# Threshold attention and an ELU feed-forward block in one kernel: two more second-FFN products split once more, ELUs of two groups held back, two quarters behind the last values, a new early order

## The chip, the cores and the metric

The kernel runs on one core of a Trainium2 chip. The metric is device time in microseconds, the median of several executions; a profiled execution beside them gives the trace. Engines are named as in the profile: PE is TensorE (matmul, and PEld its weight load), DVE is VectorE, ACT is ScalarE, POOL is GpSimd, SP is SyncE, which here only issues transfers. All arithmetic is float32.

## The reference, cut to what matters

```python
# q, k, v: (8, 8, 576, 64)
scores = q @ k^T / sqrt(64)
scores = where(scores >= max(scores) - tau, scores, -1e9)
attn = exp(scores - max(scores)); attn /= sum(attn) + 1e-9
x = (attn @ v).transpose(0, 2, 1, 3).reshape(4608, 512)
h = x @ w_in                                # 512 -> 2048
g = where(h > 0, h, exp(min(h, 0)) - 1)     # ELU
out = g @ w_out                             # 2048 -> 512
```

## The kernel before

Each of the 8 sequences has 8 heads, worked as 4 head pairs; there are 32 pairs in all. A pair's scores (L493 early, L766 later) go to PSUM, DVE takes the row maximum (L517, L773), ACT the exponential (L527, L783), DVE the mask with the row sum (L537, L787), DVE, POOL and ACT sum and normalize. The squares are transposed on DVE (L640), stored to DRAM (`there`) and fetched back in another layout (`wTa`, `wTb`, L684). The values product (L818, L826) multiplies them by v, and ACT copies it to `xt` (L432), the transposed input of the FFN.

The FFN works on groups of tokens. Both of its products are computed as seven half-size products instead of eight (a Strassen scheme), with sums of input blocks and weight blocks prepared ahead. `first_product(g, u)` (matmuls at L1444) gives one of eight pieces of h of group g; ACT copies three of the seven partial results (L1458) and two blocks of h (L1505, L1506), POOL and DVE combine, and per half c ACT takes the exponential (L1474), POOL or ACT subtracts one (L1484, L1486), and DVE finishes the ELU (L1494). `second_round(g, r)` (L1584) is the second FFN product of half the hidden columns; its left operands need sums s1 to s4 of ELU results (`sums`, L1531).

The stages in time:

- Early (0 to about 263 us): the list `EARLY` is a written-out order of steps, each with an engine or a choice of engines (`:act`, `:dve`, `:pool`), carried out by `early_tasks` and `follow`. Its names: `su` row sums, `rest` parts of the weight conversion (L280 to L321), `max`, `exp`, `mask`, `th` the softmax steps, `part`/`put` transposes by PE and their copies, `half` halves of first FFN products.
- Steady state (263 to 1036 us): for pair `pr` from `START` = 9 to 32, an agenda sorted by planned time (`at`) issues each step. `tail_step` and `wide_step` give the attention work of a pair with its planned times; between them `ffn_quarters(n)` issues n quarters of FFN work (a quarter is two matmul calls, four instructions on PE). `MOVED` shifts planned times by name ("f" or "s" for a pair with first products or second rounds beside it, then the step), `FIRST` the times of one pair, or, with the key "e:" and the number of a quarter, of the steps behind the steady state.
- The last values (about 1066 to 1071 us): the values of the last pair and their copy to `xt`, from which the last two groups, 7 and 8, start.
- The last two groups: eight first products of group 7; deep round 0; first products 0 to 3 of group 8; deep round 1; first products 4 to 7; deep rounds 2 and 3. Rounds 0 and 1 are the second FFN product of group 7 (r = 0, 1), rounds 2 and 3 of group 8.

A deep round goes through seven products m in the order `DEEP` = 0, 3, 2, 4, 1, 5, 6; with four rounds that makes 28, numbered q. Each is either plain (`plain_product`, L2020: 8 calls of 128x256 columns) or split once more by the same scheme (`deep_product`, L1958: 14 calls of 128x128). Each call is two instructions on PE in the trace. A product is plain when (r, m) is in `WHOLE`, or q is 27.

A split product needs four left sums of ELU results (`level2_sum`, L1893; s1, s2, s3, s4; s3 and for r = 0 s4 on POOL, the others on DVE, unless `ON` says otherwise) and four sums of weights (`weigh`, made ahead, kept in DRAM as `there_w` and loaded by `load_weights`, L1883). Its results leave PSUM in parts: L1970, L1977, L1980 on DVE when r = 1, partly copies on ACT when r = 0; those of a plain product by L2026 on DVE when r = 1. `between(q)` issues the sums s1 and s2 of the next product and, at some places, `later_sum` (L1876, L1878). `sums_deep` (L1864, L1866) makes sums of ELU results as soon as two ELUs are done. In both kinds of sum PE waits if they are late.

The set `patient` names first products whose ELUs are planned later than usual:

```python
patient = {(B - 1, 7), (B, 3), (B, 7)}
at(now[0] + (2.0 if c and attending[0] else 1.4) + (7.0 if deep_sums and (g, u) in patient else 0.0), lambda: elu(c), f"e{v}{c}")
```

With B = 8 these are u = 7 of group 7, which runs directly before deep round 0, u = 3 of group 8 before round 1, and u = 7 of group 8 before round 2. An ELU that has not been issued yet is also issued when its buffer is taken again by a later exponential, or when a product needs its result (`ready`).

Of the kernel before, what the change touches and what calls it, by code (L numbers as in the profile page):

```python
# [60 lines left out]
ld.tail.1.0 ld.tau.0.0:act ld.k.0.1 ld.k.0.0:act idle17@f0 ld.q.0.0 ld.k.1.0 ld.k.1.1 lw.0 lw.1 tau first.t.k.0@f0  # L61
ld.k.2.0 copy.k.0 ld.k.2.1 first.k.0.0@f2 ld.k.3.0 idle4@f0 prep.k.0.0 ld.k.3.1 first.q.0.0@f0 first.q.1.0@f2
prep.q.0.0 ld.tail.0.0 first.t.k.1@f1 sc.0 copy.k.1:dve lw.2 first.t.k.2@f0 max.0.0 copy.k.2 prep.q.1.0 first.q.2.0@f0
idle7@t max.0.1 exp.0.0 th.0.0 lw.3 first.k.1.0@f2 prep.q.2.0 th.0.1 exp.0.1 mask.0.0 rest.0:pool idle5@f0 prep.k.1.0
mask.0.1 first.t.k.3@f1 ld.vd.3.0 shift.0 sc.1 copy.k.3:dve sign.0 ld.q.1.0 shift.1 su.0 ld.q.2.0 rec.0 first.q.3.0@f0
max.1.0 norm.0.0 ld.vd.0.1 prep.q.3.0 first.k.2.0@f0 max.1.1 ld.v.1.1 exp.1.0 th.1.0 rest.1:pool ld.q.3.0
first.t.q.0@f2 exp.1.1 part.0.0@t mask.1.0 th.1.1 add.0 first.k.3.0@f1 prep.k.2.0 mask.1.1 first.t.q.1@f0 ld.v.0.0
su.1:act copy.q.0 sc.2 end.0 norm.0.1:act rec.1 shift.2 prep.k.3.0 norm.1.1 part.0.1@f2 max.2.0 sign.1 idle21@f1
rest.2:pool ld.v.0.1 max.2.1 exp.2.0 th.2.0 ld.vd.0.0 th.2.1 exp.2.1 mask.2.0 add.1 lw.4 put.0.0 mask.2.1 sign.2
norm.1.0 end.1 rest.3 sc.3 ld.v.1.0 su.2:act copy.q.1 add.2 put.0.1 lw.5 part.0.2@t turn.0 max.3.0 part.1.0@f1  # L70
ld.vd.2.1 put.0.2 landed.0 first.q.0.1@f0 max.3.1 exp.3.0 th.3.0 ld.v.3.1 first.q.1.1@f2 part.1.1@t rec.2 ld.v.2.1
th.3.1 exp.3.1 mask.3.0 norm.2.0 ld.vd.1.1 prep.q.0.1 mask.3.1 ld.vd.1.0 put.1.1 part.1.2@f0 turn.1 put.1.0 shift.3
# [12 lines left out]
exp.8.1 add.8 part.6.0@t part.7.1@f1 put.7.0 mask.8.1 part.6.1@f2 sign.7 part.7.2@f0 turn.7 su.8 put.6.0 sc.9 end.7
put.7.1 end.8 lw.11 rest.9 half.0@f1 rec.8 load.k.4 shift.9 put.6.1 max.9.0 add.9 norm.8.1:act put.7.2:dve landed.7
exp.9.0 max.9.1 part.6.2@t turn.6 th.9.0 val.3.block.1@f0 norm.8.0:act th.9.1 mask.9.0 lw.12 rest.10:pool exp.9.1
shift.10 sc.10 mask.9.1 out.3.block.1 add.10 sign.9 put.6.2:dve landed.6 sign.10 part.8.0@f0 max.10.0 su.9:act
part.8.1@t part.8.2@f2 turn.8 end.9 half.1 exp.10.0 th.10.0 rec.9 put.8.2 lw.13 put.8.1 mask.10.0 norm.9.0 put.8.0
landed.8 end.10 norm.9.1 su.10:act first.t.q.3@f2 first.t.q.2@f0 sc.11 copy.q.2 copy.q.3 shift.11 lw.14 rest.11 rec.10  # L90
norm.10.0 fexp.0.0.0 val.2.block.1@t max.11.0 max.11.1 exp.11.0 th.11.0 fmin.0.0.0 exp.11.1 out.2.block.1:dve
part.10.0@f0 th.11.1 mask.11.0 add.11 part.9.0@t put.10.0 part.9.1@f2 mask.11.1 sign.11 part.10.1@f0 turn.10 shift.12
end.11 sc.12 put.10.1 landed.10 rest.12 shift.13 lw.15 sign.12 su.11:act add.12 half.4@f0 max.12.0 put.9.0 rec.11
max.12.1 exp.12.0 th.12.0 end.12 th.12.1 rest.13 part.9.2@t turn.9 half.5 exp.12.1 mask.12.0 add.13 lw.16 put.9.2
load.q.4 put.9.1 landed.9 mask.12.1 sign.13 sc.13 elu.0.0.0 norm.11.1:act su.12 rec.12 val.0.1@t norm.12.0:act
norm.12.1 max.13.0 end.13 exp.13.0 th.13.0 fexp.0.1.0 mask.13.0 norm.11.0:act fmin.0.1.0 turn.12 su.13:act rest.14
in.0.0:pool sc.14 rest.15 in.0.1:pool rec.13 send.12 in.0.2:pool part.11.0@f1 max.14.0 half.8@f2 in.1.0:pool max.14.1
exp.14.0 th.14.0 elu.0.1.0 th.14.1 lw.17 out.0.1 put.11.0 shift.15 part.11.1@f0 shift.14 exp.14.1 part.11.2@t turn.11
half.2@f1 add.14 mask.14.0 sign.14 put.11.1 mask.14.1 landed.12 norm.13.0:act end.14 sc.15 shift.16 lw.18 put.11.2:dve
landed.11 part.13.0@f0 max.15.0 half.3 max.15.1 exp.15.0 th.15.0 add.15 su.14 sign.15 rec.14 mask.15.0 rest.16 th.15.1  # L100
part.13.1@t turn.13 end.15 exp.15.1 add.16 sc.16 put.13.0 prep.q.4 put.13.1 landed.13 half.9 sign.16 mask.15.1
load.q.5 in.1.1:pool norm.14.1:act max.16.0 in.1.2:pool su.15:act shift.17 val.1.1@t exp.16.0 th.16.0 in.2.0:pool
prep.k.4 fexp.0.0.1 insend.0 rest.18:pool norm.14.0:act mask.16.0 lw.19 rest.17 end.16 fmin.0.0.1:act add.17 su.16
rec.15 lw.20 shift.18 sc.17 out.1.1 rec.16 elu.0.0.1 norm.15.1:act norm.15.0 fexp.0.0.2 part.14.0@t max.17.1 norm.16.0
half.6@f0 put.14.0 max.17.0 in.2.1:pool fmin.0.0.2:act turn.15 exp.17.0 th.17.0 th.17.1 part.14.1@t add.18 sign.17
part.14.2@f1 turn.14 half.7 exp.17.1 send.15 mask.17.0 in.2.2:pool put.14.2 mask.17.1 elu.0.0.2 part.16.0@f1 su.17:act
sign.18 end.17 sc.18 put.16.0 rec.17 end.18 lw.21 norm.17.0:act half.10@f1 max.18.0 put.14.1 landed.14 max.18.1
landed.15 exp.18.0 th.18.0 lw.22 in.3.0 th.18.1 exp.18.1 half.11 mask.18.0 rest.19:pool in.3.1:pool mask.18.1 su.18
# [68 lines left out]
def kernel(  # L177
# [13 lines left out]
    B, H, S, D = q.shape  # L191
# [29 lines left out]
    early, late = ExitStack(), {}  # L221
# [743 lines left out]
    NP = B * NPAIR  # L965
# [414 lines left out]
    with tc.manual_schedule():  # L1380
# [42 lines left out]
        def first_product(g, u):  # L1423
            r, v = divmod(u, RU)
# [704 lines left out]
```

## Time and profile before

| | before |
|---|---|
| time, median of 3 executions (lowest to highest) | 1270.01 us (1269.47 to 1270.43) |
| profiled execution, its own time | 1268.97 us |
| span of the profile (first to last instruction) | 1266.9 us |
| busy: PE / DVE / POOL / ACT | 1249.4 / 1066.1 / 790.1 / 584.1 us |
| mean granted PE clock | 0.999 |
| PE time by line on the chain of waits | L1444 31%, L1584 23%, L766 8%, L826 8%, L1958 4%, L2020 2% |

A row of a timeline is: start, duration, engine, line, operation, tiles written <- read, shapes, count; in brackets the engine's idle time before it, and who ended it. Rows with a count above 1 join instructions that follow each other. A row by stretch gives busy time per engine within a stretch of the span. In the chain of waits each row is one link: start, length, engine, tile, line, count. Line numbers are those of the kernel before; in the kernel after they are higher by 1 (by 2 from about L1999).

### The profile page before, as it was taken

The numbers are of one execution on the slowest core, as the hardware profiler recorded it, in microseconds if no ns is written. First come the engines' busy times: TensorE is split into PE (matmuls) and PEld (weight loads), VectorE is DVE, ScalarE is ACT, GpSimd is POOL, SyncE is SP. The second block draws the span as 40 slices with busy tenths as digits, with TensorE's granted clock in tenths as the row PEclk, the third lists the DMA queues.
The fourth block names the chain that finished last, engine by engine and source line by source line (L and its number), as shares of the span: only waits on it lengthen the run. The fifth ranks groups of instructions, "written<-read, shape, count | busy, mean of one in ns | idle before, by whom it ended". The sixth has DMA issues, their size and how long they took to land.

```text
span 1266.9 us, 22594 instructions
## 1 busy us (share of the span) xinstructions
PE 1249.4 (99%) x7163; PEld 992.5 (78%) x7163; DVE 1066.1 (84%) x2330; ACT 584.1 (46%) x1271; POOL 790.1 (62%) x1144
## 2 busy tenths in 40 slices
PE   7999999999999999999999999999999999999998
PEld 6776576478788887878788878878887888888898
DVE  6998989898889979898889888988989776776776
ACT  6986755453444435352625353443535251434130
POOL 5674544586576747684767657675757474775564
PEclk9999999999999999999999999999999999999999
DMA  9568898998889887988889897988898876334433
GB/s 224 144 177 237 228 260 240 246 299 214 258 205 279 216 245 213 269 238 245 234 226 264 219 267 204 268 214 253 207 279 222 243 217 241 137 125 150 135 112 113
DMA packets 332871, 277.70 MB, mean 219 GB/s; under 512 B 201296, under 2 KB 288336, under 8 KB 332752
## 3 DMA queue, kind: packets, MB, share of 16 engines
q1 hardware_dynamic: 331760, 275.73, 77.9%
q8 instruction: 57, 0.93, 0.3%
q10 hardware_dynamic: 992, 0.53, 0.2%
q14 instruction: 62, 0.51, 0.1%
HBM read 178.85 MB, written 97.32 MB: 218 GB/s over the span
## 4 chain that ended last, share of the span: by engine, by line
PE 79%; DVE 3%; issue 0%; SPq 0%; ACT 0%; DMA 0%; POOL 0%; DVEq 0%; ACTq 0%
PE f L1444 31%; PE f L1584 23%; PE sc L766 8%; PE sc L826 8%; PE f L1958 4%; PE f L2020 2%; PE sc L818 1%; PE sc L813 1%; PE f L953 1%; DVE mx L773 0%; DVE x L640 0%; DVE w_one L787 0%; DMA there<-x 0%; DVE kT L1893 0%; DVE s L1866 0%
## 5 line engine op out<-in xcount | busy, mean ns | idle before, releaser
L773 DVE TENSOR_REDUCE mx<-sc 128x1 f32<-128x576 f32 x252 | 179.9, 750 | 35.5 <-PE sc L766 28.4
L783 ACT ACTIVATE w_one<-sc,mx 128x576 f32<-128x576 f32 x140 | 101.1, 739 | 125.6 <-DVE mx L773 104.5
L779 POOL TENSOR_SCALAR th<-mx,ntau 128x2 f32<-128x2 f32 (+1 forms) x140 | 41.7, 298 | 174.5 <-DVE mx L773 174.4
L766 PE MATMUL sc<-kT,qT 64*128 64x256 f32 (+5 forms) x896 | 126.6, 418 | 2.1 <-ACT xt L432 0.9
L766 PEld LDWEIGHTS sc<-kT,qT 64*128 64x128 f32 x896 | 99.3, 186 | 35.4 <-issue 18.9
L1444 PE MATMUL f<-xt,sw 128*128 128x256 f32 x512 | 123.8, 384 | 0.5 <-ACT xt L432 0.5
L1444 PE MATMUL f<-x,w_in_sb 128*128 128x256 f32 x512 | 122.8, 382 | 0.0
L1444 PE MATMUL f<-xt,w_in_sb 128*128 128x256 f32 x512 | 121.2, 379 | 0.5 <-DVE xt L1053 0.5
L787 DVE SCALAR_TENSOR_TENSOR w_one<-sc,th,w_one 128x576 f32<-128x576 f32 x140 | 109.7, 811 | 13.1 <-ACT w_one L783 12.9
L783 ACT ACTIVATE e<-sc,mx 128x576 f32<-128x576 f32 x112 | 82.7, 742 | 74.5 <-DVE mx L773 72.2
L640 DVE STREAM_TRANSPOSE x<-w_one 128x512 f32<-128x512 f32 (+1 forms) x140 | 100.0, 744 | 15.2 <-POOL w_one L501 10.2
L501 POOL TENSOR_SCALAR w_one<-w_one,rs 128x576 f32<-128x576 f32 x115 | 89.3, 787 | 37.3 <-DVE rs L551 37.3
L1444 PEld LDWEIGHTS f<-xt,sw 128*128 128x128 f32 x512 | 94.1, 190 | 19.5 <-issue 4.3
L1444 PEld LDWEIGHTS f<-x,w_in_sb 128*128 128x128 f32 x512 | 96.2, 190 | 16.1 <-ACT g L1505 3.6
L1444 PEld LDWEIGHTS f<-xt,w_in_sb 128*128 128x128 f32 x512 | 97.2, 190 | 14.0 <-ACT e L783 0.8
L787 DVE SCALAR_TENSOR_TENSOR e<-sc,th,e 128x576 f32<-128x576 f32 x112 | 87.8, 809 | 8.2 <-ACT e L783 7.9
L1584 PE MATMUL f<-w_out_sb,g 128*128 128x256 f32 x384 | 92.0, 382 | 0.0
L1584 PE MATMUL f<-w_out_sb,s 128*128 128x256 f32 x384 | 91.9, 382 | 0.0
L1584 PE MATMUL f<-t,s 128*128 128x256 f32 x384 | 90.7, 379 | 0.0
L501 POOL TENSOR_SCALAR e<-e,rs 128x576 f32<-128x576 f32 x92 | 67.7, 741 | 35.4 <-DVE rs L551 32.6
L1584 PEld LDWEIGHTS f<-w_out_sb,g 128*128 128x128 f32 x384 | 72.0, 190 | 12.2 <-issue 2.9
L1584 PEld LDWEIGHTS f<-w_out_sb,s 128*128 128x128 f32 x384 | 72.0, 190 | 11.8 <-issue 2.5
(344 smaller groups left out, 2902.7 us busy)
## 6 DMA issues: line engine op xcount, KB each, us to landing
there<-x SPq DMA_DIRECT2D x452, 144.0 KB, 3.9
wTb<-there SPq DMA_DIRECT2D x58, 576.0 KB, 6.2
wTa<-there SPq DMA_DIRECT2D x55, 576.0 KB, 4.8
sw<-win_sums SPq DMA_DIRECT2D x62, 384.0 KB, 4.3
t<-wout_sums SPq DMA_DIRECT2D x45, 512.0 KB, 5.2
there<-x SPq DMA_DIRECT2D x112, 80.0 KB, 1.9
wTb<-there SPq DMA_DIRECT2D x56, 160.0 KB, 3.6
wst<-in_moe_w_in_dram SPq DMA_DIRECT2D x16, 512.0 KB, 4.6
```

The source lines that it names most:

```text
L501: nc.gpsimd.tensor_scalar(wv, wv, st["rs"][:, h : h + 1], 1.0, ALU.mult, ALU.mult)
L640: nc.vector.transpose(x[:, :, c0 : c0 + nc_], src.rearrange("p (c g n) -> p g c n", c=nc_, n=T))
L766: on_banks(nc.tensor.matmul(o, qT[r, i * P : (i + 1) * P], kT[r, k0 : k0 + n], start=True, stop=True, skip_group_check=True), o)
L773: on_banks(nc.vector.tensor_reduce(st["mx"][:, h : h + 1], st["sc", h], axis=AX.XY if i == NC else AX.X, op=ALU.max, negate=True), st["sc" ...
L779: nc.gpsimd.tensor_scalar(st["th"][:, cs], st["mx"][:, cs], -1.0, ntau, ALU.mult, ALU.add)
L783: on_banks(nc.scalar.activation(st["e", h], st["sc", h], AF.Exp, bias=st["mx"][:, h : h + 1]), st["sc", h])
L787: on_banks(nc.vector.scalar_tensor_tensor(st["e", h], st["sc", h], st["th"][:, h : h + 1], st["e", h], ALU.is_ge, ALU.mult, accum_out=st[" ...
L826: on_banks(nc.tensor.matmul(o, vm[:, h, c], parts[part][:, g0:g1, h * (NC + 1) + c], start=False, stop=(c == NC - 1), skip_group_check=Tru ...
L1444: nc.tensor.matmul(loc["banks"][place], left[:, j], right[:, j], start=(begins and j == 0), stop=(j == 1), skip_group_check=True)
L1584: nc.tensor.matmul(place(m), lhs, rhs, start=(begins and v == 0), stop=(v == RU - 1), skip_group_check=True)
L1958: nc.tensor.matmul(loc["x"][place][:, :P], left[:, v], right[:, v], start=(begins and v == 0), stop=(v == 1), skip_group_check=True)
L2020: nc.tensor.matmul(loc[c][:, :HM], lefts(g, r, c, m)[:, v], rights(r, m)[:, v], start=(v == 0), stop=(v == RU - 1), skip_group_check=True)
```

## The change

1. `WHOLE` loses (1, 4): the products m = 4 of rounds 1 and 3 (q = 10 and 24) are split. Split products go from 17 to 19 of 28, plain ones from 11 to 9.
2. `patient` becomes a table: the ELUs of (7, 7) and (8, 3) are held back by 20.0 instead of 7.0, those of (8, 7) by 7.0 as before.
3. The last second round leaves two quarters (four L1584 calls, eight instructions on PE) until after the last values. As side effects two of its sums (L1531) move from POOL to DVE, and the "e:" keys of `FIRST` name other quarters than before.
4. In a split product the slots run 1, 5, 6 instead of 1, 6, 5 (5 uses s1, 6 uses s2); the load of the weight sums and `later_sum` move from slot 5 to slot 6.
5. `ON` gets nine entries that put single sums on another engine; `FIRST` gets one entry, and nine planned times in `MOVED` change.
6. `EARLY` is a new order. PE's own order in the early stage is the same; 24 steps change engine and some steps of DVE, ACT, POOL and SP change places.

In the built programs, DVE has 2044 instructions before and 2063 after, ACT 1279 and 1284, POOL 1149 in both, SP 1369 and 1374; L1958 goes from 238 to 266 calls and L2020 from 88 to 72.

```diff
 FIRST = {
-    "9:3.0": 0.61, "9:turn4": 2.44, ...
+    "9:3.0": 0.61, "9:fetch0": -3.6, "9:turn4": 2.44, ...
 ON = {
+    "L8.0.0.3": 1, "S1.3": 0, "S15.2": 0, "S16.1": 1, "S16.3": 0, "S19.3": 0, "S2.3": 0, "S5.1": 1, "S5.3": 0,
 }
-WHOLE = {(0, 0), (1, 0), (0, 4), (1, 4), (1, 5)}
+WHOLE = {(0, 0), (0, 4), (1, 0), (1, 5)}
 MOVED = {
-    ... "f20.1": 2.47, ... "f26.1": 0.42, ... "f5.1": 4.32, ... "fout1": 0.83, ... "s21.0": 0.22,
-    ... "sexp11": -0.09, ... "sfetch4": 0.31, ... "sprep1": -0.32, ... "sturn4": -1.49,
+    ... "f20.1": 3.18, ... "f26.1": -0.14, ... "f5.1": 3.93, ... "fout1": 0.47, ... "s21.0": 0.51,
+    ... "sexp11": -0.16, ... "sfetch4": -0.76, ... "sprep1": -2.36, ... "sturn4": -3.1,
 EARLY = """
-... shift.0 sc.1 copy.k.3:dve sign.0 ld.q.1.0 shift.1 su.0 ld.q.2.0 rec.0 first.q.3.0@f0 ...
+... shift.0 ld.vd.3.0 sc.1 su.0:act copy.k.3:dve sign.0 ld.q.1.0 shift.1 rec.0 rest.0 ld.q.2.0 norm.0.0 ...
...
-        patient = {(B - 1, 7), (B, 3), (B, 7)}
+        patient = {(B - 1, 7): 20.0, (B, 3): 20.0, (B, 7): 7.0}
...
-                at(now[0] + (2.0 if c and attending[0] else 1.4) + (7.0 if deep_sums and (g, u) in patient else 0.0), lambda: elu(c), f"e{v}{c}")
+                at(now[0] + (2.0 if c and attending[0] else 1.4) + (patient.get((g, u), 0.0) if deep_sums else 0.0), lambda: elu(c), f"e{v}{c}")
...
-                ffn_quarters(HALF_QUARTERS)
+                ffn_quarters(HALF_QUARTERS - (2 if pr == NP and half else 0))
...
             one = [(0.1, first), (0.15, s_(q, 2))]
-            six = [(0.1, u2), (0.15, first_too), (0.35, s_(q, 3))]
-            five = [(0.2, lambda: load_weights(q + 3, 0))] + between(q)
+            b_ = between(q)
+            five = [x for x in b_ if x[0] == 0.3]
+            six = [(0.1, u2), (0.15, first_too), (0.35, s_(q, 3)), (0.2, lambda: load_weights(q + 3, 0))] + [x for x in b_ if x[0] != 0.3]
...
-            return [slot(1, one), slot(6, six), slot(5, five)], [slot(2, [(0.1, c11)]), ...], [slot(7, seven)]
+            return [slot(1, one), slot(5, five), slot(6, six)], [slot(2, [(0.1, c11)]), ...], [slot(7, seven)]
```

More of the change, by code (lines that the diff above doesn't have):

```diff
@@ L86 @@
[L86 to L95, printed above, removed]
@@ new lines @@
+put.17.1 sign.21 part.19.1@t turn.19 in.5.0 add.22 part.17.2@f1 turn.17 half.12@f2 put.19.1 landed.19 end.21 put.17.2
+landed.17 in.5.1 in.5.2:pool val.3.1@t shift.23 insend.5 sign.23 insend.4 rest.23 lw.25 sign.22 add.23 copy.k.4:act
+end.22 prep.k.5 rest.24:pool lw.26 out.3.1 t tail.4 half.19 bmax.4.4.0 insend.2 shift.24 bexp.4.4.0 bth.4.4 add.24
+sign.24 bmask.4.4.0 idle3@f1 end.23 bsu.4.4:act wsc.4.0.0 brec.4.4 end.24 lw.27 bnorm.4.4.0:act wsc.4.0.1 insend.3
+shift.25 rest.25 lw.28 bmax.4.0.0 half.16@f1 insend.1 bmax.4.0.1 bexp.4.0.0 load.q.6 bturn.4.4 bth.4.0 sign.25
@@ L2006, in deep_product @@
             slot = lambda k, posts: (lambda: p(k), posts, SLOT)
-            return [slot(1, one), slot(6, six), slot(5, five)], [slot(2, [(0.1, c11)]), slot(4, [(0.1, c21), (0.2, lambda: load_weights(q + 3, 1))]), slot(3, three)], [slot(7, seven)]
+            return [slot(1, one), slot(5, five), slot(6, six)], [slot(2, [(0.1, c11)]), slot(4, [(0.1, c21), (0.2, lambda: load_weights(q + 3, 1))]), slot(3, three)], [slot(7, seven)]
         def plain_product(q):
```

201 lines of the change are left out of this document (103 added, 98 removed), and 18 rows, old and new, of the table MOVED.

## The prediction

> **What bounds the kernel now.** I read the page's head, then busy time by stretch, the waits of TensorE (PE), the chain of waits, and the timeline around each wait.
>
> ```profile
> span 1266.9 us, 22594 instructions
> PE 1249.4 (99%) x7163; PEld 992.5 (78%) x7163; DVE 1066.1 (84%) x2330; ACT 584.1 (46%) x1271; POOL 790.1 (62%) x1144
> ```
>
> PE is busy all but 17.5 us, so a gain can only be fewer matmul-microseconds or a PE wait that goes. Where is the idle time? The view by stretch (stretch, its length, then busy time of PE, weight load, DVE, ACT, POOL, granted clock, DMA share, GB/s):
>
> ```profile
> 0.00:27.00 27.00, 20.93 (x136) 16.01 (x136) 16.32 (x43) 17.80 (x38) 13.56 (x35) 1.00 1.01 226
> 27.00:46.00 19.00, 18.32 (x171) 13.82 (x171) 17.91 (x44) 18.39 (x37) 12.71 (x19) 1.00 0.57 167
> 46.00:115.00 69.00, 67.52 (x526) 53.45 (x522) 62.19 (x143) 60.63 (x132) 45.87 (x63) 1.00 0.68 177
> 115.00:263.00 148.00, 145.03 (x708) 88.13 (x709) 130.66 (x280) 85.20 (x164) 78.44 (x109) 1.00 0.91 246
> 263.00:1036.00 773.00, 772.98 (x4334) 622.42 (x4335) 677.43 (x1490) 342.31 (x749) 507.09 (x761) 1.00 0.87 240
> 1066.00:1072.00 6.00, 5.53 (x42) 3.11 (x42) 3.26 (x7) 1.05 (x4) 0.00 (x0) 1.00 0.78 276
> 1120.00:1143.00 23.00, 21.73 (x159) 20.20 (x158) 18.81 (x42) 5.02 (x15) 16.44 (x17) 1.00 0.34 116
> 1143.00:1167.00 24.00, 24.00 (x122) 21.34 (x121) 14.91 (x31) 10.70 (x26) 12.38 (x17) 1.00 0.48 162
> 1169.00:1192.00 23.00, 22.28 (x151) 20.50 (x150) 21.55 (x57) 1.15 (x2) 13.25 (x16) 1.00 0.29 92
> 1238.00:1258.00 20.00, 20.00 (x143) 18.94 (x143) 17.86 (x48) 0.27 (x1) 9.07 (x10) 1.00 0.36 106
> ```
>
> PE idles 6.07 + 0.68 + 1.48 + 2.97 = 11.2 us in the early stage, 0.02 in the long steady state (263 to 1036), 0.47 behind the last values, 1.27 in deep round 0 (1120 to 1143), 0.72 in round 1 (1169 to 1192) and none in round 3. So the new planned times of the steady state can gain nothing; they can only lose.
>
> **The change, part by part.**
>
> *Two more products split* (L1958 instead of L2020, m = 4 in rounds 1 and 3). Rates, from the chain of waits (start, time, engine, line, count):
>
> ```profile
> 1249.98 2.68 PE f L1958 x24
> 1252.65 1.73 PE f L2020 x8
> ```
>
> A plain product issues 8 calls, each two instructions on PE: 16 at 1.73/8 = 216 ns, 3.46 us. A split one issues 28 at 2.68/24 = 112 ns, 3.13 us. Two of them save 2 x 0.33 = 0.67 us. A rule against it stands in the Trainium skill, "TensorE: Matmul & The Clock Gate", section "Back-to-back issue gap": sustained spacing is set by weight load and matmul together, about 81 ns at 128 columns and 131 ns at 512, so halving the width does not halve the time. The trace disagrees for 256 to 128: 216 ns to 112. What it would cost is the last rival.
>
> *ELUs held back 20 instead of 7* (u = 7 of group 7, u = 3 of group 8). Round 0, DVE and PE (start, time, engine, line, operation, tiles, shapes; in brackets the idle time before it and who ended it), then round 1:
>
> ```profile
> 1128.52 1.64 DVE L1494 SCALAR_TENSOR_TENSOR wTb<-km,wTb 128x512 f32<-128x512 f32 x1
> 1130.60 0.97 DVE L1866 TENSOR_TENSOR s<-wTb 128x256 f32<-128x256 f32 x1
> 1131.49 0.41 DVE L1893 TENSOR_TENSOR kT<-g 128x256 f32<-128x256 f32 x1
> 1131.83 0.41 DVE L1864 TENSOR_TENSOR e<-s,wTb 128x256 f32<-128x256 f32 x1
> 1132.16 0.68 DVE L1494 SCALAR_TENSOR_TENSOR wTa<-ge,wTa 128x512 f32<-128x512 f32 x1
> 1132.77 0.41 DVE L1893 TENSOR_TENSOR kT<-kT,g 128x256 f32<-128x256 f32 x1
> ...
> 1131.62 0.61 PE L1958 MATMUL f<-t,g 128*128 128x128 f32 x4
> 1133.23 1.16 PE L1958 MATMUL f<-x,kT 128*128 128x128 f32 x8 [1.00 <-DVE kT L1893]
> ...
> 1180.46 0.68 DVE L1494 SCALAR_TENSOR_TENSOR g<-km,g 128x512 f32<-128x512 f32 x1
> 1181.06 0.41 DVE L1893 TENSOR_TENSOR kT<-kT,wTb 128x256 f32<-128x256 f32 x1
> 1181.53 1.16 PE L1958 MATMUL f<-x,kT 128*128 128x128 f32 x8 [0.57 <-DVE kT L1893]
> ```
>
> In both rounds the second left sum (kT, L1893), which PE waits for, comes right behind an ELU (L1494) and the sums of h that the ELU sets off (L1866, L1864). These are for the next round of the same group's columns, a first-product stage later; held 20 they land in that stage (1143 to 1167), where DVE is busy 14.91 of 24. Lateness is more than the idle shown: four matmuls from 1131.62 take 0.45, so the next was due at 1132.07 and came 1.16 late, 0.16 more than the 1.00 shown, because a stopped PE drains its last matmul before it counts as idle. PE restarts five times in the two rounds, idle 1.27 + 0.72 = 1.99, so late by 1.99 + 5 x 0.16 = 2.8. DVE work ahead of these sums falls by at least 1.64 + 0.97 + 0.41 + 0.68 = 3.7 in round 0, more than any single wait. I take **-2.8** (bounds -2.8 and 0).
>
> *New DVE work.* A split product in rounds 1 and 3 adds on DVE three left sums (L1893), one L1970, six L1980, one L1977, and drops two L2026; the fourth sum goes to POOL or DVE as ON says. Groups on DVE in round 3 (busy, mean ns, idle before):
>
> ```profile
> L1980 DVE TENSOR_TENSOR ot<-f,wTb 128x128 f32<-128x128 f32 x10 | 2.8, 286 | 0.6 <-PE f L1958 0.5
> L1893 DVE TENSOR_TENSOR kT<-kT,e 128x256 f32<-128x256 f32 x2 | 1.7, 862 | 0.1
> L2026 DVE TENSOR_TENSOR kT<-f,kT 128x256 f32<-128x256 f32 x2 | 0.8, 410 | 0.0
> ```
>
> With 0.41 for an undisturbed L1893 (1131.49), and the two forms without a row here at the price of their shape (L1970 as L1980, L1977 as L2026): 3 x 0.41 + 0.29 + 6 x 0.29 + 0.41 - 2 x 0.41 = 2.9 by durations; successive rows start 0.07 sooner than that (1131.49 to 1131.83 is 0.34), nine more instructions give 0.6 back, so 2.2 us. Round 1 loses ELU work of about that size. Round 3 doesn't: 17.86 + 2.2 = 20.1 us of DVE in the 19.67 us that PE would need. So DVE is full and at least 0.4 comes out as waits; the same L1893 at 862 ns shows that a sum can take 0.45 longer. I take **+0.8** (0.4 and one stretched sum). Bounds: 0, if the tail after the last matmul takes the excess, and 3.1, if all six new L1893 stretch by 0.45 (2.7 + 0.4). The order 1, 5, 6 in place of 1, 6, 5 gives s2 one slot of four matmuls (0.45 us) more and s1 as much less; s1 is issued first and is the earlier of the two, so I take nothing for it; if s1 were the late one, it costs up to 0.45 in a round, within these bounds.
>
> *Two quarters behind the last values.* The chain, and the switch:
>
> ```profile
> 1041.75 24.37 PE f L1584 x112
> 1067.24 4.05 PE sc L826 x32
> ...
> 1069.37 1.90 PE L826 MATMUL sc<-wTa,vm 128*64 128x256 f32 x16
> 1071.31 0.37 ACT L432 COPY xt<-sc 128x256 f32<-128x256 f32 x1 [1.03 <-PE sc L826]
> 1071.74 1.56 PE L1444 MATMUL f<-xt,sw 128*128 128x256 f32 x6 [0.47 <-ACT xt L432]
> ...
> 1055.31 0.43 SPq L684 DMA_DIRECT2D wTb<-there  x1
> ```
>
> PE ends the values, the copy to xt (0.37) follows, PE waits 0.47 and is late by 0.47 + 0.16 = **0.63**. Eight L1584 matmuls (24.37/112 x 8 = 1.74 us) now fill that gap. Their sums (L1531) go from POOL to DVE, which has 3.26 of 6 busy there: hidden, else at most the 0.63 again. The values start 1.74 earlier, at 1041.75 + 24.37 - 1.74 = 1064.4; the last fetch was issued at 1055.31. No row shows the landing of this one; PE waits for no fetch now, so it lands by 1066.1 at the latest, and the step then loses up to 1.7. I take no loss.
>
> *Early stage.* PE's order stays the same; 24 entries change engine (seven row sums leave DVE for ACT, four weight conversions go from ACT to POOL) and some are reordered. The largest wait that I can follow:
>
> ```profile
> 61.02 0.71 ACT L280 ACTIVATE wst<-wst 128x512 f32<-128x512 uint32 x1
> 62.23 1.36 ACT L527 ACTIVATE e<-sc,mx 128x576 f32<-128x576 f32 x2
> 64.18 0.41 PE L554 MATMUL f<-ident,w 128*64 128x128 f32 x2 [0.55 <-ACT wTb L432]
> ```
>
> L280 there goes to POOL, so ACT reaches the exponentials up to 0.71 sooner and the 0.55 can go. Elsewhere ACT gets work in front of its exponentials. Much of the 11.2 us is start-up that no order removes. I take **-0.7**, one such wait with its 0.16; bounds -2.0 (three such) and +1.0 (ACT late once before two of PE's restarts).
>
> *Steady state, ON, SP.* 0: PE never waits there, and each moved step has other work of PE in front. SP gets one more store and four more half loads, three products ahead of their use. No row prices them; the step that waits would be one L1958 start, 0 to 0.45.
>
> Sum: -0.67 - 2.8 + 0.8 - 0.63 - 0.7 = -4.0. The profiled execution took 1268.97 (span 1266.9 and 2.07 around it), 1.04 below the median of 1270.01. So 1268.97 - 4.0 = 1264.97 as profiled, **1266.0** as a median.
>
> **Rivals.**
> (a) DVE becomes the bound of rounds 1 and 3: the new sums cost 3.1, not 0.8, so 1268.3. For it: 17.86 of 20 busy, and L1893 at 862 ns; against it: PE had no wait at all in round 3.
> (b) The held ELUs do not clear the rounds (they are also forced when their buffer is taken again), or other DVE work takes their place ahead of kT: the 2.8 stays, 1268.8. Against: the first-product stage that takes the buffer begins after the round.
> (c) Slower: a wait that repeats in the steady state. In one stage ACT has this order now:
>
> ```profile
> 474.70 0.37 ACT L1506 COPY g<-f 128x256 f32<-128x256 f32 x1 [0.49 <-PE f L1444]
> 474.97 0.63 ACT L1474 ACTIVATE ge<-g 128x512 f32<-128x512 f32 x1
> 475.63 0.63 ACT L1486 ACTIVATE ge<-ge 128x512 f32<-128x512 f32 x1
> ```
>
> The change puts L1474 and L1486 ahead of the L1506 copy, which frees a PSUM bank. The copy comes up to 1.26 - 0.49 = 0.77 later. It decides if PE needs that bank within 0.77 of now; fully so, 12 such stages cost 12 x 0.55 = 6.6: 1272.6. Against it: three banks rotate, and PE shows 0.02 idle in 773 us.
> (d) The 128-wide matmuls of the new products stay at 216 ns (weight load busy 18.94 of 20): 28 x 0.216 - 3.46 = 2.6 each, 5.2 in place of -0.67: 1271.9. By the skill's 81 to 131 ns, an estimate of some 180 ns, it would be 1269.8. Against it: 24 in 2.68.
>
> **How the numbers follow.** Forecast 0.60; (a) 0.16, (b) 0.12, (c) 0.10, (d) 0.02. The likeliest one's own range is 1264.2 to 1267.6 (early stage -2.0 to +0.5, DVE 0 to 1.6). To leave out no more than 0.2 it reaches over (a) and (b): 1264.0 to 1269.5. A measurement of this kernel tells 0.2% (2.5 us) from no change: faster is below 1267.5, slower above 1272.5. Faster: 0.57 of the forecast's, 0.09 of (a) and (b) where they come halfway: 0.66. Slower: (c) fully and a little of (d): 0.08. Same: 0.26.
>
> **What would show it.** Right: L1584 x8 between the last values and L1444 with no idle; L1494 absent from rounds 0 and 1, and kT's sum no longer ending PE's waits; 28 L1958 per new product in 3.13; PE idle in round 3 below 1. Wrong: PE idle above 0.1 between 263 and 1036; L1893 as the releaser in round 3 for over 1.5 us; early stage idle above 12; a fetch as releaser of the last values.

## The result, and the profile after

| | before | after |
|---|---|---|
| median (lowest to highest, 9 executions each) | 1269.47 us (1268.44 to 1270.43) | 1266.24 us (1265.8 to 1266.88) |
| ratio, with its 95% interval | | 0.9976 [0.9965, 0.9986] |
| span of the profile | 1266.9 us | 1264.1 us |

The change makes the kernel 3.2 us faster; the forecast was 1266.0. The page of the kernel after, its head:

```profile
span 1264.1 us, 22671 instructions
PE 1248.2 (99%) x7187; PEld 993.1 (79%) x7187; DVE 1075.3 (85%) x2349; ACT 583.7 (46%) x1276; POOL 787.1 (62%) x1144
```

PE has 24 more instructions and 1.2 us less to do; its idle time went from 17.5 to 15.9 us, DVE gained 9 us. The view by stretch (columns as in the prediction; stage boundaries have moved, so the late stretches lie 2 to 4 us earlier; only the last is the same window as before, though round 3 now ends 3.6 us earlier):

```profile
0.00:27.00 27.00, 21.97 (x145) 16.80 (x146) 17.92 (x45) 20.23 (x43) 13.51 (x35) 1.00 0.92 223
...
263.00:1036.00 773.00, 773.00 (x4339) 622.10 (x4337) 676.00 (x1489) 341.90 (x749) 502.33 (x761) 1.00 0.87 240
1063.00:1071.00 8.00, 8.00 (x54) 5.36 (x53) 6.10 (x14) 1.11 (x5) 0.73 (x1) 1.00 0.61 210
1118.00:1140.00 22.00, 22.00 (x164) 21.02 (x163) 17.30 (x40) 5.03 (x15) 13.72 (x16) 1.00 0.36 121
1165.00:1188.00 23.00, 22.77 (x167) 21.47 (x166) 21.53 (x62) 1.15 (x2) 14.65 (x18) 1.00 0.31 107
1238.00:1258.00 20.00, 19.49 (x138) 18.09 (x137) 17.93 (x51) 0.00 (x0) 10.18 (x13) 1.00 0.22 70
```

The steady state is still without a wait, the switch to the last groups and round 0 have none left, round 1 has 0.23 of idle time, and round 3, which had none, now has 0.51 (also with the window moved by 3.6 us, to 1234.4 to 1254.4). The waits of PE from 1060 us on (what waited, for whom: us in total, times, longest) name another releaser than before, the copies of results out of PSUM (L1981) and no longer the sums kT:

```profile
PE f L1959 <- DVE qT L1981: 0.4, 2, 0.2
PE f L1959 <- DVE wTb L1981: 0.3, 1, 0.3
```

Cut at the starts of PE's stages, the trace gives the following lengths in us. "Early" is the start of the last matmul of the early stage that waits (for `xt`, 0.47 in every run); "switch" runs from the start of the last long row of L1584 to the first L1444 of group 7; "tail" from the end of the last matmul to the end of the span. Between these columns every run has the same lengths within 0.02 (48.35 for group 7's first products with the two quarters moved and 48.45 without, save one run told of below; 25.52 for each of group 8's two stages), and the steady state, up to the switch, takes 778.7 to 779.5.

| kernel | early | switch | round 0 | round 1 | rounds 2, 3 | tail | span |
|---|---|---|---|---|---|---|---|
| before | 262.88 | 30.06 | 23.21 | 22.75 | 45.90 | 3.79 | 1266.9 |
| after | 261.47 | 29.62 | 21.45 | 21.93 | 46.89 | 4.61 | 1264.1 |
| q24_plain | 261.71 | 29.62 | 21.45 | 21.93 | 45.89 | 3.94 | 1262.7 |
| q10_plain | 261.67 | 29.62 | 21.45 | 21.52 | 46.89 | 4.57 | 1263.8 |
| both_plain | 262.39 | 29.62 | 21.45 | 21.52 | 45.90 | 4.19 | 1263.9 |
| patient_7 | 261.49 | 29.62 | 23.26 | 24.85 | 46.90 | 4.61 | 1268.8 |
| only_patient | 263.04 | 30.06 | 21.21 | 21.52 | 45.90 | 3.81 | 1263.8 |
| early_before | 263.03 | 29.62 | 21.44 | 21.93 | 46.89 | 4.66 | 1266.0 |
| quarters_14 | 262.07 | 30.06 | 21.45 | 22.52 | 46.90 | 4.60 | 1267.1 |
| on_empty | 261.34 | 29.62 | 21.40 | 21.93 | 46.92 | 4.62 | 1264.0 |
| sum_on_dve | 262.15 | 29.62 | 21.45 | 21.92 | 46.58 | 4.63 | 1264.5 |
| slots_165 | 261.43 | 29.62 | 21.20 | 21.24 | 45.98 | 4.58 | 1262.4 |
| slots_165_b | 261.51 | 29.62 | 21.20 | 21.20 | 45.98 | 4.48 | 1262.3 |
| slots_165_q24 | 261.48 | 29.62 | 21.20 | 21.20 | 46.30 | 3.93 | 1262.5 |

From before to after: up to the switch -1.47, the switch -0.44 and the first products behind it -0.10, round 0 -1.76, round 1 -0.82, rounds 2 and 3 **+0.99**, the tail **+0.82**; together -2.8. So 4.6 us were won and 1.8 given back at the end. The experiments ask who gave them back, and which edit won the rest.

### The profile page after: what moved, and what is told of

Read it like the earlier page. It is cut to its first block, busy times and chain, and to the rows that moved or that the text cites. A ratio compares the mean times of both kernels' runs of the same rounds, so it can differ in the third digit from the quotient of the medians.

```text
span 1264.1 us, 22671 instructions
## 1 busy us (share of the span) xinstructions
PE 1248.2 (99%) x7187; PEld 993.1 (79%) x7187; DVE 1075.3 (85%) x2349; ACT 583.7 (46%) x1276; POOL 787.1 (62%) x1144
## 4 chain that ended last, share of the span: by engine, by line
PE 92%; DVE 4%; ACT 2%; issue 1%; DMA 1%; SPq 0%; POOL 0%; DVEq 0%; ACTq 0%; POOLq 0%
PE f L1445 31%; PE f L1585 23%; PE sc L767 9%; PE sc L827 9%; PE f L1959 4%; PE f L2022 2%; PE f L954 2%; PE f L886 2%; PE f L914 2%; PE sc L494 2%; PE sc L819 1%; PE sc L814 1%; PE f L555 1%; PE sc L713 1%; DVE mx L774 1%
## 5 line engine op out<-in xcount | busy, mean ns | idle before, releaser
L780 POOL TENSOR_SCALAR th<-mx,ntau 128x2 f32<-128x2 f32 (+1 forms) x140 | 45.9, 328 | 189.4 <-DVE mx L774 189.3
L1445 PE MATMUL f<-xt,sw 128*128 128x256 f32 x512 | 123.5, 384 | 0.0
L1445 PE MATMUL f<-x,w_in_sb 128*128 128x256 f32 x512 | 122.8, 382 | 0.0
L1445 PE MATMUL f<-xt,w_in_sb 128*128 128x256 f32 x512 | 121.2, 379 | 0.5 <-DVE xt L1054 0.5
L1445 PEld LDWEIGHTS f<-x,w_in_sb 128*128 128x128 f32 x512 | 96.2, 190 | 16.1 <-ACT g L1506 3.6
L1445 PEld LDWEIGHTS f<-xt,sw 128*128 128x128 f32 x512 | 94.3, 190 | 18.2 <-issue 4.8
L1445 PEld LDWEIGHTS f<-xt,w_in_sb 128*128 128x128 f32 x512 | 97.2, 190 | 14.0 <-ACT e L784 0.8
L1585 PEld LDWEIGHTS f<-t,s 128*128 128x128 f32 x384 | 73.0, 190 | 9.9
```

The costliest lines, as they stand in the source:

```text
L780: nc.gpsimd.tensor_scalar(st["th"][:, cs], st["mx"][:, cs], -1.0, ntau, ALU.mult, ALU.add)
L1445: nc.tensor.matmul(loc["banks"][place], left[:, j], right[:, j], start=(begins and j == 0), stop=(j == 1), skip_group_check=True)
L1585: nc.tensor.matmul(place(m), lhs, rhs, start=(begins and v == 0), stop=(v == RU - 1), skip_group_check=True)
```

## The experiments

Times are the median of the run with its ratio to the kernel before and the 95% interval, all from runs on one chip per group. Where a tenth counts, the stage lengths above carry the argument: kernels with the same edits in a round agree there within 0.05, while the early stage scatters by 1.1 us between kernels with the same order (261.34 to 262.39), and the tail by 0.25 between two with the same round 3 (q24_plain, both_plain).

### Was it the splits? q24_plain, q10_plain, both_plain

```diff
# q24_plain (q10_plain with 10 for 24)
-            if (q // 7 == rounds_begun[0] or rounds_begun[0] == 2) and q < 27 and (rounds...
+            if (q // 7 == rounds_begun[0] or rounds_begun[0] == 2) and q < 27 and q != 24 and (rounds...
-            follows = q + 1 < 28 and (pos ...
+            follows = q + 1 < 28 and q + 1 != 24 and (pos ...
-                if (rounds[x][1], DEEP[q % 7]) in WHOLE or q == 27:
+                if (rounds[x][1], DEEP[q % 7]) in WHOLE or q in (24, 27):
# both_plain
-WHOLE = {(0, 0), (0, 4), (1, 0), (1, 5)}
+WHOLE = {(0, 0), (0, 4), (1, 0), (1, 4), (1, 5)}
```

> The changed kernel, with product 24 (m = 4 of round 3) plain again; product 10 stays split. Theory A (DVE is full in round 3, so the split there costs more than its 0.33 us of PE time): the three restarts of PE in round 3 (late 0.45 + 0.48 + 0.55 = 1.3 with the slow second matmul) go, rounds 2 and 3 return from 46.89 to 45.9 us, and the stretch from the last matmul to the end shrinks from 4.61 to about 3.8; in all 1.8 us less, span near 1262.3, time near 1264.5. Theory B (the loss in round 3 comes from the new slot order or from ON, not from the split): the restarts stay, and the span grows by the 0.33 of PE time to 1264.4.

> The changed kernel, with product 10 (m = 4 of round 1) plain again; product 24 stays split. Round 1 has 0.55 us of PE lateness left after the change, at two restarts around product 10. Theory A (the split fills DVE in round 1 too, but the held ELUs made room): round 1 goes from 21.93 to between 21.7 and 22.1 us, the split is worth next to nothing there, span within 0.3 of 1264.1. Theory B (the split is a gain in round 1, and the restarts come from somewhere else): round 1 grows by 0.33 to 22.26.

> The changed kernel with products 10 and 24 plain, as in the kernel before; all other edits stay. If each split loses by itself and they don't influence each other, round 1 is 21.52 (as with product 10 alone plain) and rounds 2 and 3 are 45.89 with a tail of 3.94 (as with product 24 alone plain): span 1264.1 - 0.41 - 1.0 - 0.67 = 1262.0, time near 1264.1, faster than the changed kernel. If the splits pay 0.33 each somewhere else, the span is 1262.7 or more.

q24_plain took 1265.14 us (0.9962 [0.9949, 0.9974]), q10_plain 1266.15 (0.9971 [0.996, 0.9983]), both_plain 1265.69 (0.997 [0.9958, 0.9981]). Without product 24 split, rounds 2 and 3 return to 45.89 and the tail to 3.94: theory A's numbers. Product 10 plain makes round 1 shorter by 0.41, a third case that neither theory gave: the split loses there too. The two add up in the rounds (21.52 and 45.90), but the span of both_plain missed the 1262.0 expected: its early stage ended 0.9 later than after's, its steady state took 0.7 longer, with waits of 0.23 and 0.10 near 280 us, and its tail was 0.25 longer than that of q24_plain. The first two lie ahead of everything that the edit changes, for the sums of weights that it saves belong to the last second round, from 1056 us on.

So the waits hang on the splits. That DVE is full, as theory A says, did not follow from this; the next run showed another reason, the order of the slots.

### Or the order of the slots? slots_165, slots_165_b

In the kernel after, PE and then DVE around the first loss in round 3 (timeline; a bracket is idle time and who ended it), and POOL:

```profile
1243.22 0.68 PE L1959 MATMUL f<-x,wTb 128*128 128x128 f32 x4
1243.73 0.61 PE L1959 MATMUL f<-w_out_sb,s 128*128 128x128 f32 x4
1244.57 1.16 PE L1959 MATMUL f<-w_one,kT 128*128 128x128 f32 x8 [0.22 <-DVE qT L1981]
...
1241.46 1.45 DVE L1894 TENSOR_TENSOR kT<-qm 128x256 f32<-128x256 f32 x1
1242.84 0.28 DVE L1981 TENSOR_TENSOR wTb<-f,wTb 128x128 f32<-128x128 f32 x1
...
1243.90 0.41 DVE L1894 TENSOR_TENSOR kT<-kT,s 128x256 f32<-128x256 f32 x1
1244.23 0.47 DVE L1981 TENSOR_TENSOR qT<-f,wTb 128x128 f32<-128x128 f32 x2
...
1241.36 1.27 POOL L1877 TENSOR_TENSOR vm<-wTa 128x512 f32<-128x512 f32 x1
```

What PE waits for at 1244.57 is no sum: kT is ready 0.3 us before, at 1243.90 + 0.41. The profile names the pair of copies at 1244.23, which empty banks of an earlier product: the first of them, 0.28 long like the one at 1242.84, ends at 1244.51. In the order 1, 5, 6, slot 5 is the first to want the third bank of its product, and it comes one slot (0.45 us) sooner than in 1, 6, 5. Also, the sum kT<-qm is now issued ahead of the copies on DVE and not behind some of them.

```diff
# slots_165
-            return [slot(1, one), slot(5, five), slot(6, six)], ...
+            return [slot(1, one), slot(6, six), slot(5, five)], ...
-            b_ = between(q)
-            five = [x for x in b_ if x[0] == 0.3]
-            six = [(0.1, u2), (0.15, first_too), (0.35, s_(q, 3)), (0.2, lambda: load_weights(q + 3, 0))] + [x for x in b_ if x[0] != 0.3]
+            six = [(0.1, u2), (0.15, first_too), (0.35, s_(q, 3))]
+            five = [(0.2, lambda: load_weights(q + 3, 0))] + between(q)
# slots_165_b, besides
-    ... "e:139.1": 0.46, ...
```

> The changed kernel with the slots of a split product in the order 1, 6, 5 of before. Theory A (the new order gives the second left sum, which is the later one, 0.45 us more, and this keeps restarts away): PE waits for kT or for the second sum again in rounds 0, 1 or 3, 0.2 to 0.45 us at each of one to four products, span 1264.5 to 1265.5. Theory B (with the held ELUs the order doesn't matter): each round within 0.1 us of 21.45, 21.93 and 46.89.

> The changed kernel with the slots of a split product in the order 1, 6, 5 of before, and without the entry of FIRST that names a step by its place in slot 6 (e:139.1). Theory A (slot 5 takes the third bank of its product, which an earlier product's last result copies, L1981, give free; run one slot of 0.45 us earlier, it meets them): the waits on L1981 in rounds 1 and 3 go, rounds take 21.2, 21.2 and 46.0 us, span 1262.0 to 1262.7, time near 1264.5, although both products are split. Theory B (only the second left sum and its order count): round 1 takes 21.9 again, rounds 2 and 3 46.9, span 1264 or more.

slots_165 took 1264.41 us (0.9962 [0.9948, 0.9976]). Both theories missed it: the old order is not slower by waits for sums, nor equal; it is faster (one such wait, of 0.15 in round 2, is told of at the end). In this first kernel, though, the entry "e:139.1" of `FIRST` fell on another step, so that one left sum s2 of round 1 was computed from the sum s1 of the product before, and its output is not the reference's. slots_165_b, without that entry, took 1264.25 us (0.9958 [0.9944, 0.9971]): 21.20, 21.20 and 45.98, theory A's numbers, with both products split. The same stretch of it:

```profile
1243.18 0.61 PE L1959 MATMUL f<-w_out_sb,s 128*128 128x128 f32 x4
1243.63 1.06 PE L1959 MATMUL f<-w_one,kT 128*128 128x128 f32 x8
...
1241.38 0.41 DVE L1978 TENSOR_TENSOR wTb<-f,ot 128x256 f32<-128x256 f32 x1
1241.71 0.89 DVE L1894 TENSOR_TENSOR wTa<-wTb,kT 128x256 f32<-128x256 f32 x1
1242.53 0.41 DVE L1894 TENSOR_TENSOR kT<-qm 128x256 f32<-128x256 f32 x1
...
1243.39 0.47 DVE L1981 TENSOR_TENSOR qT<-f,wTb 128x128 f32<-128x128 f32 x2
```

Slot 1 starts at 1243.18, the copies qT at 1243.39, 0.21 behind it; the first is done at 1243.67, the second at 1243.86. Slot 5 is now third, due at 1244.08, so the bank is empty; as second it would have been due at 1243.63, just too early. In the kernel after, slot 1 starts at 1243.73, the copies 0.50 behind it, and slot 5 is due at 1244.18, before they have even begun. So both halves of the edit show: the slot is worth 0.45 us, the later copies 0.29. How the loss divides between them wasn't tried. By this comparison the new slot order, with the steps moved along with it, costs 0.25 + 0.73 + 0.91 us in the rounds, 1.9 in all; the 0.13 in the tail is within the tail's scatter.

With product 10 plain, round 1 takes 21.52 in either order (both_plain has 1, 5, 6, only_patient 1, 6, 5). It is 21.20 here, so with the old order the split of product 10 pays its 0.32.

### slots_165_q24: does the split of product 24 then pay?

The kernel before this one with product 24 plain, the edit of q24_plain.

> The kernel before this one, with product 24 plain besides. If the split of product 24 pays its 0.33 us once the slots stand 1, 6, 5, rounds 2 and 3 grow from about 46.0 to 46.2 or shrink less than 0.2, and only the tail (4.6 to 3.9, since DVE has 2.2 us less to do before the last results) is won: span 0.4 to 0.7 shorter, near 1261.8, time near 1263.9. If DVE is full in round 3 whatever the slots, rounds 2 and 3 shrink by more, to 45.6. If the tail doesn't hang on the split, the span grows by 0.2 to 0.4.

It took 1264.26 us (0.9957 [0.9944, 0.9969]), the same as slots_165_b. Rounds 2 and 3 grow by 0.32, the split's gain exactly; the tail shrinks by 0.55. By stage lengths that is 0.23 won, less than the 0.4 expected, and the runs can't tell it from nothing. So with the old slots the split in round 3 gains on PE and gives the gain back behind the last matmul. Where: the last additions on POOL, and with them the last stores on ACT's queue, come later with respect to PE's end. Kernel after, POOL, the last PE row and the stores:

```profile
1253.90 1.46 POOL L1912 TENSOR_TENSOR ot<-ot,kT 128x256 f32<-128x256 f32 x2 [3.09 <-DVE kT L1911]
...
1255.86 3.62 PE L2022 MATMUL f<-w_out_sb,e 128*128 128x256 f32 x16
...
1258.32 2.73 ACTq L947 DMA_DIRECT2D out_dram<-ot  x4
```

and the kernel before:

```profile
1256.56 1.46 POOL L1911 TENSOR_TENSOR ot<-ot,kT 128x256 f32<-128x256 f32 x2 [2.91 <-DVE kT L1910]
...
1259.46 3.62 PE L2020 MATMUL f<-w_out_sb,e 128*128 128x256 f32 x16
...
1261.34 2.73 ACTq L946 DMA_DIRECT2D out_dram<-ot  x4
```

L1912 starts 5.6 us before the last matmul ends (1259.48), L1911 before the change 6.5 (1263.08). The stores on ACT's queue end 1.6 after it instead of 1.0. The two kernels that differ by this split alone show the same: 5.6 and 1.5 us in slots_165_b, 6.5 and 1.0 in slots_165_q24.

### sum_on_dve: why one sum took 1.45 us

```diff
 ON = {
-    "L8.0.0.3": 1, ...
+    "L8.1.1.2": 0, "L8.0.0.3": 1, ...
```

> The changed kernel with one sum of round 3 (vm, L1877, 128x512, 1.27 us on POOL from 1241.36) moved from POOL to DVE, where it stands behind kT's second sum and ahead of the result copies (L1981) that PE waits for at 1244.57. Theory A (a DVE sum of two SBUF operands stands still while POOL runs): kT's first sum takes 0.41 in place of 1.45 us, which is more than the 0.60 that L1877 takes on DVE, so DVE reaches those copies 0.4 us sooner; the restarts at 1243.22 and 1244.57 (0.24 and 0.48) shrink to 0.3 in all, rounds 2 and 3 take 46.5 us or less. Theory B (DVE is only full; the 1.45 is a wait for data): the copies come 0.6 later, and rounds 2 and 3 take 47.4 or more.

1266.27 us (0.9979 [0.9969, 0.9988]); rounds 2 and 3 take 46.58, near theory A's 46.5 and far from 47.4. The same rows on DVE:

```profile
1242.14 0.42 DVE L1894 TENSOR_TENSOR kT<-qm 128x256 f32<-128x256 f32 x1
...
1243.99 0.69 DVE L1877 TENSOR_TENSOR vm<-wTa 128x512 f32<-128x512 f32 x1
1244.59 0.48 DVE L1981 TENSOR_TENSOR qT<-f,wTb 128x128 f32<-128x128 f32 x2
```

With the POOL sum gone, kT<-qm takes 0.42, not 1.45. In the kernel after it had started 0.10 behind POOL's L1877 and ended at 1242.91, 0.28 after that one (1242.63), as if it had stood still until then. All left sums on DVE in the two kernels (L1893 before, L1894 after) behave so: the 43 that start while a POOL instruction runs end 0.27 to 0.29 us after it and take 0.42 to 1.45; the other 53 take 0.41 to 0.43. The 862 ns that the prediction read in round 3 before are the mean of one of each kind, 1.31 and 0.42. This is what the Trainium skill says, "SBUF — State Buffer", section "Who interferes with whom": a DVE instruction with two SBUF inputs contends with a GpSimd instruction that reads SBUF, and the lock on the ports that they share is exclusive. The trace agrees, by the 1.03 us. So moving work onto the busier engine made it faster here; rounds 2 and 3 got 0.3 us shorter.

### The ELUs: patient_7 and only_patient

```diff
# patient_7 (kernel after); only_patient is the kernel before with 20.0 for the first two
-        patient = {(B - 1, 7): 20.0, (B, 3): 20.0, (B, 7): 7.0}
+        patient = {(B - 1, 7): 7.0, (B, 3): 7.0, (B, 7): 7.0}
```

> The changed kernel, with all ELUs held back by 7.0 as before. Theory A (the ELUs and the sums behind them stood ahead of the left sums on DVE): deep round 0 returns from 21.45 to 23.2 us, round 1 from 21.93 to 22.7 or more, since the new split has its DVE work there as well; span 2.5 to 3.5 us longer, 1266.6 to 1267.6. Theory B (the slot order or ON took the waits away): rounds 0 and 1 stay within 0.3 us of 21.45 and 21.93.

> The kernel before with the ELUs held back by 20 as its only change. By the prediction's working: rounds 0 and 1 take 23.2 - 1.76 = 21.45 and 22.75 - 1.04 = 21.7 us, span 1264.1, time 2.8 less than before. If the 4.7 us that the ELUs cost in the changed kernel come from the ELUs alone, and not from their meeting the new slots and the split, it is 4.7 less: span 1262.2.

patient_7: 1271.44 us (1.0012 [1.0003, 1.0021]), slower than before. Round 0 loses 1.8 as theory A says, but round 1 2.9, more than three times the 0.8 expected. only_patient: 1266.46 us (0.9974 [0.9963, 0.9984]); round 0 goes from 23.21 to 21.21, round 1 from 22.75 to 21.52, in all 3.2, between the two numbers expected and near the first; the early stage was 0.2 late. So this one edit alone is as fast as the whole change. In patient_7 the same ELUs cost 4.7. The extra 1.5 us appears in round 1, so the ELUs seem to meet the new split and the new slots there; neither was taken out of patient_7 by itself. Its DVE and PE rows:

```profile
1176.47 0.68 DVE L1495 SCALAR_TENSOR_TENSOR g<-ge,g 128x512 f32<-128x512 f32 x1
...
1177.60 0.96 DVE L1867 TENSOR_TENSOR s<-g 128x256 f32<-128x256 f32 x1
...
1179.35 0.68 DVE L1495 SCALAR_TENSOR_TENSOR g<-km,g 128x512 f32<-128x512 f32 x1
...
1178.29 0.61 PE L1959 MATMUL f<-w_out_sb,wTa 128*128 128x128 f32 x4
1180.33 0.68 PE L1959 MATMUL f<-x,wTb 128*128 128x128 f32 x4 [1.43 <-issue]
```

PE stands 1.43 us where the kernel after has no wait.

### early_before, quarters_14, on_empty

```diff
# early_before: EARLY as in the kernel before
# quarters_14
-                ffn_quarters(HALF_QUARTERS - (2 if pr == NP and half else 0))
+                ffn_quarters(HALF_QUARTERS)
# on_empty
-    "L8.0.0.3": 1, "S1.3": 0, "S15.2": 0, "S16.1": 1, "S16.3": 0, "S19.3": 0, "S2.3": 0, "S5.1": 1, "S5.3": 0,
```

> The changed kernel, with the early order of before. Theory A (the new order alone shortens the early stage): PE's last restart of that stage, at 261.47 in the changed kernel, comes at 262.9 again as in the kernel before, and the span grows by 1.4 to 1265.5. Theory B (the gain there is scatter between executions or comes from the steady state's planned times): it stays within 0.3 us of 261.47.

> The changed kernel with all 14 quarters ahead of the last values, as before. Theory A (the two quarters cover PE's wait for the last copy to xt): the stretch from the last second round's start to the first L1445 of group 7 returns from 29.62 to 30.06 us, a wait of 0.47 on the copy of xt stands in front of it, nothing else moves: 0.44 us. Theory B (the names of the planned steps behind shift with the quarters, so deep rounds change too): rounds move by more than 0.2.

> The changed kernel without the nine entries that put single sums on another engine. Theory A (moving five of POOL's sums to DVE and three of DVE's to POOL only evens the two out): rounds 0 to 3 each within 0.3 us. Theory B (POOL's sums were late in rounds 0 and 2, and moving them to DVE is what took the restart at 1136 and 1140 away): round 0 takes 0.2 to 0.6 us more, with POOL as the releaser, and rounds 2 and 3 likewise; span 1264.3 to 1265.3.

early_before: 1268.24 us (0.999 [0.9981, 0.9999]); the last restart comes at 263.03, as theory A says. The three kernels with the old order stand at 262.88 to 263.04, the eleven with the new one at 261.34 to 262.39, so the new order is worth 1.3 us by the means of the two groups; the times of the two runs differ by 2.0.

quarters_14: 1268.33 us (0.9989 [0.998, 0.9998]). Theory A's 0.44 is there (switch 30.06, and 0.47 in front of the first L1445), but theory B holds too: round 1 takes 0.59 more, and group 7's first products 48.96 instead of 48.35, with a new wait:

```profile
1071.61 1.56 PE L1445 MATMUL f<-xt,sw 128*128 128x256 f32 x6 [0.47 <-ACT xt L433]
...
1092.84 1.35 PE L1445 MATMUL f<-xt,w_in_sb 128*128 128x256 f32 x5 [0.24 <-ACT w L1459]
```

The planned times of `FIRST` and the sums are tied to the number of quarters issued; taking the two back alone leaves the rest tuned to another count. Its span is 3.0 us over that of after: 0.44 in the switch, 0.61 and 0.59 in these two, 0.6 of early scatter and 0.7 in the steady state.

on_empty: 1265.97 us (0.9975 [0.9966, 0.9984]); every round within 0.05. With the slots 1, 5, 6 the nine entries do nothing that a run can show.

`MOVED` of before was not tried by itself. PE's 773.00 busy of 773 says what it did for PE.

## Why the prediction was right, point by point

The total was right (1266.0 against 1266.24), and so was the largest term in its mechanism. That the total is so close is luck in good part. As profiled, the forecast was 1264.97 and the execution took 1265.96, so 3.0 us were won (2.8 by the span) and not 4.0: the slots took back 2.3 that were not in the sum, while the ELUs won 0.4 and the early order 0.8 more than forecast. The other 0.8 is in the step from profiled to median, where the prediction added 1.04 and 0.28 was right.

- **ELUs, -2.8.** Right. Alone it gave 3.2. The 0.4 more are second matmuls: behind each of the five restarts the next matmul comes another 0.07 to 0.10 late, which the working had left out. Only two of the five restarts named the sums kT (late 1.16 and 0.73); the other three (0.20, 0.40 and 0.31) named another releaser or none, and the working counted them in without a reason of their own. They went as well: only_patient has no restart left in rounds 0 and 1. The rows of after that answer to round 0's: no ELU is left between the sums, and PE goes from 1129.61 to 1130.06 without a stop:

```profile
1127.28 1.33 DVE L1894 TENSOR_TENSOR kT<-g 128x256 f32<-128x256 f32 x1
1128.64 0.83 DVE L1894 TENSOR_TENSOR kT<-kT,g 128x256 f32<-128x256 f32 x1
...
1129.61 0.61 PE L1959 MATMUL f<-t,g 128*128 128x128 f32 x4
1130.06 1.06 PE L1959 MATMUL f<-x,kT 128*128 128x128 f32 x8
```

- **The splits, -0.67.** Right: 0.32 each on PE (round 1 with the old slots 21.52 to 21.20, rounds 2 and 3 46.30 to 45.98). The matmul of 128 columns takes about half of that of 256, as the rows said and the rule of the Trainium skill ("TensorE: Matmul & The Clock Gate", section "Back-to-back issue gap") did not.
- **New DVE work, +0.8 as waits in round 3.** Right in size (0.55), wrong in place: with the old slots PE waits nowhere for it in round 3, and it appears in the tail. The prediction had named the tail only as the way to 0, but a longer tail is time as well. The 2.2 us of new work are about right: over round 3 (the second half of rounds 2 and 3) DVE is busy 20.46 us after against 18.51 before and 18.14 in q24_plain. But the sum 20.1 against 19.67 had put all of it into a window of 20 us that ends 5 us before PE does. The same window, moved by 3.6 us, holds 18.86, and DVE was not full.
- **Slot order, 0.** This is the step that failed. The prediction weighed only whether s1 or s2 is late, and left out what else the order decides: which bank a slot needs, and when DVE's copies out of it are due. Against rounds without any restart it cost 0.24 in round 0, 0.73 in round 1 and 1.31 in round 3 (three restarts at 1243.22, 1244.57 and 1249.59 with their second matmuls). In round 2 it spares the restart of 0.4 that slots_165_b has (its rows stand at the end of this section), so that rounds 2 and 3 differ by only 0.91. The bound of 0.45 a round was too small.
- **Two quarters, -0.63.** Measured 0.54 (0.44 in the switch and 0.10 behind it). The values found their last fetch landed, and nothing waits:

```profile
1066.18 1.90 PE L827 MATMUL sc<-wTa,vm 128*64 128x256 f32 x16
1068.01 1.99 PE L1585 MATMUL f<-w_out_sb,s 128*128 128x256 f32 x8
1069.84 1.46 PE L1445 MATMUL f<-xt,sw 128*128 128x256 f32 x6
```

- **Early stage, -0.7.** Measured 1.4 in these two traces, and not where the working had it. The wait of 0.55 that was to go is still there, and so is the L280 (now L281) on ACT in front of it; the working had put one of the moved conversions down to the wrong row:

```profile
59.75 0.70 ACT L281 ACTIVATE wst<-wst 128x512 f32<-128x512 uint32 x1
...
62.91 0.41 PE L555 MATMUL f<-ident,w 128*64 128x128 f32 x2 [0.55 <-ACT wTb L433]
```

The time is won in the first 27 us. In the kernel before:

```profile
6.03 0.63 PE L554 MATMUL f<-ident,w_out_sb 128*128 128x128 f32 x4 [0.38 <-DMA w_out_sb<-in_k_dram]
...
12.73 0.51 PE L493 MATMUL sc<-x 64*128 64x288 f32 x2 [0.69 <-DVE w L537]
...
26.57 0.33 PE L554 MATMUL f<-ident,w 128*128 128x128 f32 x1 [1.04 <-ACT x L426]
```

and after:

```profile
5.36 0.66 PE L555 MATMUL f<-ident,w_out_sb 128*128 128x128 f32 x4
...
11.82 0.51 PE L494 MATMUL sc<-x 64*128 64x288 f32 x2
...
25.10 0.33 PE L555 MATMUL f<-ident,w 128*128 128x128 f32 x1 [1.04 <-ACT x L427]
```

The wait for the load and the wait for the mask are gone; the same matmul that came at 26.57 comes at 25.10, 1.47 sooner, and nothing further is won after that (262.88 to 261.47). In the eleven kernels with the new order it comes at 24.98 to 26.03, in the three with the old one at 26.57 to 26.66, so most of the scatter, too, arises ahead of it. That the loads' new order in the first microseconds is the cause is read from these rows; it was not tried alone.

- **Steady state, ON: 0.** Right (773.00 of 773; on_empty).

With the measured sizes, from the lengths above: ELUs -3.2, splits -0.65, slots +2.3 in the rounds, tail +0.8, quarters -0.54, early -1.47: -2.8, the change of the span. Had the slot order been priced, and nothing else corrected, the forecast would have been 1268.3. None of the rivals came true: (a) and (b) named 1268.3 and 1268.8 for DVE work and ELUs that stay, (c) needed waits in the steady state, and (d) a matmul rate that the runs refute. In size (a) came close: rounds 1 and 3 and the tail lost 0.73 + 1.31 + 0.82 = 2.9, against its 3.1, but to the slots and the tail and not to the sums alone.

**A version that beats both:** the change with the slots 1, 6, 5 (slots_165_b), 1264.25 us against 1266.24 and 1269.4 (0.9958 of the kernel before, the change 0.9976). It still has one restart of its own (idle 0.14 at 1224.05, late 0.31, and its second matmul 0.10) that neither the kernel before nor only_patient has. Its rows show why:

```profile
1224.05 1.16 PE L1959 MATMUL f<-w_one,kT 128*128 128x128 f32 x8
1220.19 1.33 DVE L1495 SCALAR_TENSOR_TENSOR wTb<-ge,wTb 128x512 f32<-128x512 f32 x1
1223.59 0.41 DVE L1894 TENSOR_TENSOR kT<-kT,g 128x256 f32<-128x256 f32 x1
1219.52 1.45 POOL L1879 TENSOR_TENSOR s<-g,s 128x512 f32<-128x512 f32 x1
```

The sum kT is done at 1224.00, and PE follows. This is s2, wanted one slot earlier in the order 1, 6, 5: the very wait that the new order takes away, and the kernel after has no restart there. DVE comes to it late because, among other sums, the ELU at 1220.19 took 1.33 us beside POOL's L1879 (0.68 in only_patient, where that sum runs on DVE). L1879 is on POOL by the entry "L8.0.0.3" of `ON`. So taking that entry out with the old order may win 0.4 more; this was not tried.

## What to carry to other kernels

When the order of accumulating matmuls changes, ask two questions of each slot: is its operand ready, and is its PSUM bank empty; the copies that empty the banks stand in a queue too. Price an edit in the presence of the others: the split of product 10 loses 0.41 us with one slot order and gains 0.32 with the other, and late ELUs cost 3.2 us alone and 4.7 beside the other edits. Work that is off PE's path shows up behind the last matmul if it does not show up before.

## What was unexpected in the hardware

A restart of PE costs more than its idle time shows: an idle of 0.22 us was a lateness of 0.38, and the second matmul came another 0.10 late. And a DVE sum of two SBUF operands that started during a POOL instruction ended only 0.28 us after it, and took 1.45 us instead of 0.42 at worst, so DVE can be relieved by giving it more work.
